# Two attention units to a TensorE visit, a second way of decoding three more weight pieces, and a new table of ranks

## The chip, the cores and the metric

The kernel runs on one core of one Trainium2 chip. The metric is the device time of one execution in microseconds (us), as the median of several executions. An execution's profile gives a span, which runs from the program's first instruction to its last; what lies around the span adds some two microseconds to the time. Five engines run their own instruction streams in order: TensorE (PE), VectorE (DVE), ScalarE (ACT), GpSimd (POOL) and SyncE (SP), which issues the DMAs. Weight loads of TensorE are shown as PEld.

## What is computed

The reference has two stages. The first is softmax attention with a mask: a query sees the first `n_global` keys and its own last `n_local` keys. The second is a mixer: one small network across tokens, then one across channels, each with a residual.

```python
# batch, heads, seq, head_dim = 4, 8, 768, 64;  n_global, n_local = 8, 96
scores = scale * np.matmul(q, k.transpose(0, 1, 3, 2))
keep = is_global | is_local
scores = np.where(keep, scores + bias[None], -1000000000.0)
a = np.exp(scores - np.max(scores, axis=-1, keepdims=True))
a = a / (np.sum(a, axis=-1, keepdims=True) + 1e-09)
attn = np.matmul(a, v)
# the attention output, heads side by side: x[batch, 768, 512]
h = np.maximum(x.transpose(0, 2, 1) @ w_tok1, 0.0) @ w_tok2     # 768 -> 256 -> 768
u = x + h.transpose(0, 2, 1)
out = u + np.maximum(u @ w_ch1, 0.0) @ w_ch2                    # 512 -> 1536 -> 512
```

All arrays are float32 except the four weight matrices, which arrive as 64-bit floats and have to be turned into 32-bit ones on the chip.

## The kernel before

**Units.** The attention is cut into 48 units, 12 to a batch. A unit `v` is two heads (`e` = 0, 1) and 256 query rows. Its place in the batch gives `j` = 0, 1 or 2, the third of the sequence, four units each. Because of the mask a unit with `j` = 0 meets 256 keys in all, and one with `j` = 1 or 2 meets 384. The steps of a unit are planned in `pair` (L389):

- `load` brings the unit's packed q, k and v into one of four ring buffers (SP), and `q` scales q (POOL from the second batch on).
- `S` makes the scores (PE, tile `sp`): eight passes in the trace, with a contraction of only 64 rows, so that the two heads use the two halves of the array's rows ("64*128").
- `max` adds the bias and finds row minima of the negated scores (DVE), `exp` is the exponential (ACT), `sum` and `inv` are the reciprocal, `norm` multiplies (POOL).
- For units before the twentieth, `T` transposes on PE (tile `tp`) and `back` copies the result out of PSUM. From the twentieth on (`FAR`), `split` (DVE) sorts 16-bit halves apart, `turn` is a DMA transpose issued by SP, and `join` (DVE or ACT) sorts the halves together again.
- `V` multiplies with the values (PE, tile `op`), eight passes for `j` = 0 and twelve otherwise, with the two heads in the two halves of the array's columns ("128*64"); `put` copies to `x` (ACT).

**Token mixing** of a batch (`tokens`, L543) takes all of its units. In the third and fourth batch each of six row blocks `s` goes through `xs` (DVE), `xt` (a DMA transpose), `xw` (DVE), `nh` (ACT), `nl` (DVE) and `J` (PE, tile `pj`). After the sixth come `jh` (ACT) and `jl` (DVE) for two halves, and then eight steps `U` (PE, tile `pu`), each followed by `ua`, `uh` and `ul`, which make the high and low part of `u`.

**Channel mixing** (`channel`, L660) is most of TensorE's work: for each batch 24 steps `F` (tile `hp`, twelve matmuls of 384 columns) and 24 steps `G` (tile `acc`, twelve matmuls, planned as two halves `G..0` and `G..1`), 12 for each half of the sequence. Each product is made of three matmuls of high and low parts. `fh` (ACT) and `fl` (DVE) stand between `F` and `G`.

**Weights** (`weights`, L288) come in 30 pieces of 512 columns, six for the token network and 24 for the channel network; step `F` with number f below 12 needs pieces up to 6+2f, step `G` up to 7+2f. A piece is decoded by `down` (ACT), then either `shift`, `upper`, `lower` (three on DVE), or, for a piece number from `BYTES` on, `last` (ACT), `ends` and `lower` (two on DVE); then `high` (ACT) and `low` (POOL or DVE).

**Order.** No engine's order is written out. `Plan` (L95) is a list scheduler that runs when the program is built: each step has a planned cost, the steps it waits for, buffers and PSUM banks it takes and gives, and a rank (`rank`, L762). When an engine is free in the plan, it takes the ready step of lowest rank; TensorE adds a penalty (`TURN`) when the form of the matmuls changes. The steps are then recorded in this order, and on the chip each engine runs in it. So a changed rank, cost or rule moves steps on all engines. The channel mixing of batch b−1 is what TensorE does between the attention visits of batch b; the channel mixing of the last batch has nothing beside it.

```python
 512  [f"load{v}"] if v > 1 else [], r - 8, ["q"])
 ...
 515  add(f"S{v}", "pe", 0.86 if j else 0.65, scores, ...
 540  add(f"V{v}", "pe", 0.86 if j else 0.65, values, ...
```

Every operation is recorded through one helper (`InOrder`, L197), so that nearly all rows of the profile say L205, and tiles tell them apart.

Of the kernel before, what the change touches and what calls it, by code (L numbers as in the profile page):

```python
# [21 lines left out]
B, H, S, D = 4, 8, 768, 64  # L22
# [6 lines left out]
NF = FF // P  # L29
# [13 lines left out]
DOWN = 2.0 ** -112  # L43
BYTES = 12

# [168 lines left out]
class Fast:  # L214
# [3 lines left out]
    def __init__(self, ctx, tc, early, pk, nb, w1, w2, wc1, wc2, out):  # L218
# [8 lines left out]
        def pool(name, bufs, **kw):  # L227
            return ctx.enter_context(tc.tile_pool(name=name, bufs=bufs, **kw))

        const = self.const = pool("const", 1)  # L230

        self.ring = early.slots + [const.tile([P, 1024], F32, tag=f"r{i}", name=f"e{i}") for i in range(RING - 3)]
        self.prep = pool("prep", 2)
        self.soft = pool("soft", 8)
# [13 lines left out]
        self.A, self.Z = {}, {}  # L248
        self.plan = Plan(dict(w=2 * NF, raw=AHEAD, t=3, p=6, mix=4, nat=3, q=1, x=8, u0=8, u1=8, hl=6), BUSY,
                         dict(dve=self.dve, act=self.act, pool=self.pool))  # L250
# [138 lines left out]
    def pair(self, v):  # L389
# [122 lines left out]

        add(f"S{v}", "pe", 0.86 if j else 0.65, scores, ([f"q{v}"] if v else []) + ([f"ul{b - 1}7"] if b > 1 else []), r,
            [("sp", v, 0), ("sp", v, 1)], ["q"], "rows")
        for e in range(2):
            add(f"max{v}{e}", "dve", 0.7 if j else 0.57, lambda e=e: maxima(e), [f"S{v}"] + ([f"max{v}0"] if e else []),
                r - 10, wp if e == 0 else [], [("sp", v, e)])
            add(f"exp{v}{e}", "act", 1.0 if j else 0.89, lambda e=e: exps(e), [f"max{v}{e}"], r)
# [511 lines left out]
```

## Time and profile before

| | us |
|---|---|
| median of three executions | 616.7 (616.03 to 617.36) |
| the profiled execution | 617.54 |
| its span | 615.7 |

| engine | busy us | share of the span |
|---|---|---|
| DVE | 359.4 | 58% |
| ACT | 275.2 | 45% |
| POOL | 209.6 | 34% |

A row of the profile gives the engine, the operation, the tile that it writes and those it reads, the number of instructions and their time. In the timeline the first two columns are the start and the duration in us. Ends of matmuls are modelled by the profiler and overlap their successors, so the distance between starts is what tells the pace of TensorE. Idle time that an engine spent before an instruction stands in brackets, with what ended it.

### The profile page before, as it was taken

Reading aid. Unit: us, or ns where it says so; the run is one execution under the profiler, and the core shown is the slowest. Engines: PE = TensorE matmul, PEld = TensorE weight load, DVE = VectorE, ACT = ScalarE, POOL = GpSimd, SP = SyncE. Lnnn points to the kernel's source line nnn. Section 1 sums busy time; section 2 is a strip of 40 time slices with the busy share of each in tenths; the row PEclk is TensorE's granted clock in tenths of the full one; section 3 lists DMA queues with packets and bytes.
Section 4 is the critical chain, followed back from the end, with each engine's and each line's share of the span. In section 5 each row is a group of like instructions: output and inputs, shape, how many; then the busy total and the mean of one; then the engine's idle time right before and its main releaser. Section 6 shows DMA issues by size and latency. Waiting matters only on the chain.

```text
span 615.7 us, 10478 instructions
## 1 busy us (share of the span) xinstructions
PE 597.7 (97%) x3730; PEld 543.1 (88%) x3730; DVE 359.4 (58%) x921; ACT 275.2 (45%) x736; POOL 209.6 (34%) x319
## 2 busy tenths in 40 slices
PE   5899999899999999999999999999999999999996
PEld 3577798899998999888989999898988999999996
DVE  4999999986453417557774466676655354113112
ACT  5999968864362205446652333355423231111110
POOL 4898665773130204434321034362222124000000
PEclk9999999999999999999999999999999999999999
DMA  7971571613352001667965103457541301001001
GB/s 252 400 241 33 192 253 28 248 36 120 84 107 84 1 0 52 124 150 148 206 149 96 38 27 77 122 137 164 162 78 35 61 14 39 0 1 53 0 1 56
DMA packets 84028, 62.63 MB, mean 102 GB/s; under 512 B 69760, under 2 KB 73984, under 8 KB 83968
## 3 DMA queue, kind: packets, MB, share of 16 engines
q1 hardware_dynamic: 83968, 61.88, 37.1%
q8 instruction: 31, 0.51, 0.4%
q14 instruction: 29, 0.24, 0.1%
HBM read 38.80 MB, written 6.29 MB: 73 GB/s over the span
## 4 chain that ended last, share of the span: by engine, by line
PE 81%; DVE 7%; POOL 6%; issue 3%; DMA 1%; ACT 1%; SPq 0%; DVEq 0%; POOLq 0%
PE acc L205 29%; PE hp L205 29%; PE sp L205 6%; PE pj L205 5%; PE op L205 5%; PE pu L205 5%; POOL pp L205 3%; DVE t L205 2%; DVE w L205 2%; POOL wc L205 2%; PE tp L205 1%; DMA p<-r 1%; DVE pp L205 1%; DMA e<-pk 1%; PE xtp L205 1%
## 5 line engine op out<-in xcount | busy, mean ns | idle before, releaser
L205 PE MATMUL hp<-uh,wc 128*128 128x384 f32 x768 | 210.6, 336 | 2.3 <-POOL wc L205 1.8
L205 PE MATMUL acc<-hh,wc 128*128 128x384 f32 x768 | 198.9, 339 | 0.0
L205 PEld LDWEIGHTS hp<-uh,wc 128*128 128x128 f32 x768 | 139.6, 188 | 5.6 <-POOL wc L205 2.8
L205 PEld LDWEIGHTS acc<-hh,wc 128*128 128x128 f32 x768 | 136.6, 188 | 9.0 <-issue 8.4
L205 ACT ACTIVATE hh<-hp 128x384 fp32r<-128x384 f32 x96 | 46.9, 489 | 206.9 <-PE hp L205 194.8
L205 PE MATMUL acc<-hl,wc 128*128 128x384 f32 x384 | 128.8, 336 | 0.4 <-DVE hl L205 0.2
L205 PE MATMUL hp<-ul,wc 128*128 128x384 f32 x384 | 128.4, 334 | 0.0
L205 DVE SCALAR_TENSOR_TENSOR hl<-hp,hh 128x384 fp32r<-128x384 f32 x96 | 53.0, 552 | 127.8 <-ACT hh L205 125.8
L205 POOL TENSOR_SCALAR p<-p,st 128x256 f32<-128x256 f32 (+1 forms) x132 | 74.3, 581 | 69.2 <-DVE st L205 53.0
L205 DVE COPY r<-p 128x1024 uint16<-128x1024 uint16 (+1 forms) x90 | 65.0, 732 | 37.8 <-DMA p<-r 17.6
L205 ACT ACTIVATE p<-p,st 128x256 f32<-128x256 f32 (+1 forms) x132 | 63.6, 485 | 21.5 <-DVE st L205 21.5
L205 PEld LDWEIGHTS acc<-hl,wc 128*128 128x128 f32 x384 | 72.1, 188 | 1.0 <-DVE hl L205 1.0
L205 PEld LDWEIGHTS hp<-ul,wc 128*128 128x128 f32 x384 | 72.1, 188 | 0.0
L205 POOL TENSOR_TENSOR ul<-x,uh 128x384 fp32r<-128x384 f32 x25 | 26.9, 1085 | 103.6 <-ACT uh L205 82.9
L205 POOL TENSOR_SCALAR qs<-e,sc 128x256 f32<-128x256 f32 x36 | 22.1, 615 | 106.2 <-DMA e<-pk 71.7
L205 PE MATMUL sp<-e,qs 64*128 64x256 f32 (+1 forms) x304 | 39.3, 387 | 0.2 <-POOL qs L205 0.2
L205 POOL TENSOR_TENSOR wc<-t,wc 128x512 fp32r<-128x512 f32 x20 | 32.1, 1612 | 17.3 <-ACT wc L205 17.3
L205 POOL TENSOR_SCALAR pp<-pp,st 128x256 f32<-128x256 f32 (+1 forms) x60 | 35.8, 613 | 4.3 <-DVE st L205 4.2
L205 ACT COPY r<-p 128x1024 uint16<-128x1024 uint16 (+1 forms) x22 | 29.1, 1322 | 10.3 <-DMA p<-r 6.4
L205 PEld LDWEIGHTS sp<-e,qs 64*128 64x128 f32 x304 | 25.8, 193 | 8.3 <-issue 4.3
L205 ACT ACTIVATE pp<-pp,st 128x256 f32<-128x256 f32 (+1 forms) x60 | 28.5, 484 | 2.5 <-DVE st L205 2.5
L205 ACT COPY x<-op 128x256 f32<-128x256 f32 (+1 forms) x64 | 18.6, 319 | 24.4 <-PE op L205 24.1
(99 smaller groups left out, 779.9 us busy)
## 6 DMA issues: line engine op xcount, KB each, us to landing
w<-wc SPq DMA_DIRECT2D x24, 512.0 KB, 5.3
e<-pk SPq DMA_DIRECT2D x24, 512.0 KB, 3.9
out<-o SPq DMA_DIRECT2D x32, 192.0 KB, 1.9
e<-pk SPq DMA_DIRECT2D x13, 384.0 KB, 3.6
unit<-pk SPq DMA_DIRECT2D x8, 512.0 KB, 9.5
w<-w SPq DMA_DIRECT2D x6, 512.0 KB, 9.8
p<-r SPq DMA_TRANSPOSE x56, 3.1
unit<-pk SPq DMA_DIRECT2D x2, 384.0 KB, 3.6
```

What stands on the lines that cost most here:

```text
L205: ins = getattr(self.engine, name)(*args, **kw)
```

## The change

The change has five parts.

1. `TWINS = 24`: from unit 24 on, which is the third batch, an even unit's `S` and the following odd unit's `S` become one visit. The even one waits for both units' `q` and takes all four PSUM banks, and the odd one waits only for it, with rank −1000, so that it comes right behind. The same is done with `V`: the even unit's waits for all four `join` steps of the two units, and the odd one follows. To keep the odd unit's steps in a fixed order behind the even one's, `max`, `split`, `turn` and `join` of the odd unit wait for those of the even one.
2. Scaled queries get three buffers (`prep`, `q=2` in the plan) in place of two (`q=1`).
3. `BYTES` goes from 12 to 9: pieces 9, 10 and 11 are decoded by `last`, `ends` and `lower` in place of `shift`, `upper` and `lower`.
4. The planned cost of `lower`, `LOWER`, goes from 1.05 to 1.3.
5. The ranks are set anew: pairs, weights and channel steps.

```diff
+TWINS = 24
-BYTES = 12
+BYTES = 9
...
-        self.prep = pool("prep", 2)
+        self.prep = pool("prep", 3)
...
-        self.plan = Plan(dict(w=2 * NF, raw=AHEAD, t=3, p=6, mix=4, nat=3, q=1, x=8, u0=8, u1=8, hl=6), BUSY,
+        self.plan = Plan(dict(w=2 * NF, raw=AHEAD, t=3, p=6, mix=4, nat=3, q=2, x=8, u0=8, u1=8, hl=6), BUSY,
...
+        twins = [v] if v < TWINS else [v, v + 1] if v % 2 == 0 else []
...
-        add(f"S{v}", "pe", 0.86 if j else 0.65, scores, ([f"q{v}"] if v else []) + ([f"ul{b - 1}7"] if b > 1 else []), r,
-            [("sp", v, 0), ("sp", v, 1)], ["q"], "rows")
+        add(f"S{v}", "pe", 0.86 if j else 0.65, scores,
+            ([f"q{x}" for x in twins if x] + ([f"ul{b - 1}7"] if b > 1 else [])) if twins else [f"S{v - 1}"], r if twins else -1000,
+            [("sp", x, e) for x in twins for e in range(2)], ["q"], "rows")
...
-            add(f"max{v}{e}", ..., [f"S{v}"] + ([f"max{v}0"] if e else []),
+            add(f"max{v}{e}", ..., [f"S{v}"] + ([f"max{v}0"] if e else [] if twins else [f"max{v - 1}1"]),
...
-                add(f"turn{v}{e}", "sp", 1.9, lambda e=e: turned(e), [f"split{v}{e}"], -1000)
+                add(f"turn{v}{e}", "sp", 1.9, lambda e=e: turned(e), [f"split{v}{e}"] + ([] if twins else [f"turn{v - 1}{e}"]), -1000)
...
-        add(f"V{v}", "pe", 0.86 if j else 0.65, values, [f"{late}{v}0", f"{late}{v}1"], r - 10,
-            [("op", v)] + (["w"] if v < H // 2 else ["x"] if b and j < 2 else []), give, "columns")
+        xs = len(twins) * (["w"] if v < H // 2 else ["x"] if b and j < 2 else [])
+        add(f"V{v}", "pe", 0.86 if j else 0.65, values, [f"{late}{x}{e}" for x in twins for e in range(2)] or [f"V{v - 1}"],
+            r - 10 if twins else -1000, [("op", x) for x in twins] + xs, give, "columns")
...
-        return 40.0 + 12.0 * at[0] if at[0] < 6 else 100 + 10 * at[0]
+        return 40.0 + 12.0 * at[0] if at[0] < 6 else 100 + 8 * at[0]
...
-UPPER, LOWER, LOW = 0.85, 1.05, dict(dve=0.64, pool=1.45)
+UPPER, LOWER, LOW = 0.85, 1.3, dict(dve=0.64, pool=1.45)
```

What the new table of ranks and the new rules make of the order is seen in the built programs. The rows are an engine's instructions in order, without times; one more line at the file's top makes L205 into L206.

The first place is TensorE at the first visits of the third batch. `e_58`, `e_59` and `e_60` are the ring buffers of units 24, 25 and 26. Before:

```order
L205 MATMUL acc<-hl,wc 128x384
L205 MATMUL sp<-e_58,qs 128x128 x2
L205 MATMUL sp<-e_58,qs 128x256 x2
L205 MATMUL acc<-hh,wc 128x384 x2
L205 MATMUL acc<-hl,wc 128x384
L205 MATMUL acc<-hh,wc 128x384 x2
L205 MATMUL acc<-hl,wc 128x384
L205 MATMUL sp<-e_59,qs 128x128 x2
L205 MATMUL sp<-e_59,qs 128x256 x2
L205 MATMUL sp<-e_60,qs 128x128 x2
L205 MATMUL sp<-e_60,qs 128x256 x2
```

And of the change:

```order
L206 MATMUL hp<-uh,wc 128x384
L206 MATMUL sp<-e_58,qs 128x128 x2
L206 MATMUL sp<-e_58,qs 128x256 x2
L206 MATMUL sp<-e_59,qs 128x128 x2
L206 MATMUL sp<-e_59,qs 128x256 x2
L206 MATMUL acc<-hh,wc 128x384 x2
```

Unit 25's scores now stand directly behind unit 24's. Counted over the third and fourth batch, the attention takes 24 visits of TensorE in the new order, twelve for scores and twelve for values, and no visit holds both.

The second place is TensorE at the end of the token mixing of the third batch. `e_216` is the ring buffer of unit 35, the batch's last. Before, `V35` is followed by `G440`, `G441`, `F46`, `G450`, `G451` and `F47`; from the last row of `F47` on:

```order
L205 MATMUL hp<-uh,wc 128x384
L205 MATMUL pj<-ph,w1h 128x512
...
L205 MATMUL pj<-pl,w1h 128x512
L205 MATMUL acc<-hh,wc 128x384 x2
L205 MATMUL acc<-hl,wc 128x384
...
L205 MATMUL acc<-hl,wc 128x384
L205 MATMUL pu<-w2h,ph 128x384
```

Of the change, from `V35` on:

```order
L206 MATMUL op<-r,e_60 64x128 x4
L206 MATMUL op<-r,e_216 64x256 x2
L206 MATMUL op<-r,e_216 64x128 x4
L206 MATMUL hp<-uh,wc 128x384
...
L206 MATMUL acc<-hl,wc 128x384
L206 MATMUL pj<-ph,w1h 128x512
...
L206 MATMUL pj<-pl,w1h 128x512
L206 MATMUL pu<-w2h,ph 128x384
```

Before, the 18 matmuls of `G460`, `G461` and `G470` stand between `J25` and `U20`. Now all channel steps of the second batch stand ahead of `J23`: `F47`, `G460`, `G461`, `G470` and `G471` are all that is left between `V35` and `J23`, and nothing stands between `J23`, `J24`, `J25` and `U20`.

The third place is VectorE at the decoding of pieces 23 and 24. The rows that write `w` are `ends`, those that write `t` from `t` and `w` are `lower`. Before, where `w_1546` is piece 23 and `w_1612` piece 24:

```order
L205 SCALAR_TENSOR_TENSOR w_1546<-w_1546 128x512
L205 SCALAR_TENSOR_TENSOR t_1636<-t_1636,w_1546 128x512
L205 SCALAR_TENSOR_TENSOR hl<-hp,hh 128x384
L205 SCALAR_TENSOR_TENSOR w_1612<-w_1612 128x512
L205 SCALAR_TENSOR_TENSOR t_1660<-t_1660,w_1612 128x512
```

Of the change, where `w_1566` is piece 23 and `w_1586` piece 24:

```order
L206 SCALAR_TENSOR_TENSOR w_1566<-w_1566 128x512
L206 SCALAR_TENSOR_TENSOR t_1652<-t_1652,w_1566 128x512
L206 SCALAR_TENSOR_TENSOR hl<-hp,hh 128x384
L206 TENSOR_SCALAR st<-st 128x4
L206 RECIPROCAL st<-st 128x4
L206 SCALAR_TENSOR_TENSOR w_1586<-w_1586 128x512
L206 ISA p,st<-sp,be 128x256
...
L206 TENSOR_TENSOR wc<-t_1652,wc 128x512
L206 SCALAR_TENSOR_TENSOR t_1668<-t_1668,w_1586 128x512
```

The maxima (`ISA`) of units 17, 18 and 19, which stood at the last piece or behind it, now stand among pieces 22 to 26, and `low` of pieces 23, 24 and 26 has moved from POOL to DVE. In the other direction `low` of pieces 9 and 14 has moved from DVE to POOL. On TensorE `T17`, `S19`, `T18`, `V17`, `V18` and `G100`, which stood behind `F11`, now stand ahead of it.

More of the change, by code (lines that the diff above doesn't have):

```diff
@@ L511, in pair @@
         wp = ["w"] if wide else ["p", "p"]
-        add(f"S{v}", "pe", 0.86 if j else 0.65, scores, ([f"q{v}"] if v else []) + ([f"ul{b - 1}7"] if b > 1 else []), r,
-            [("sp", v, 0), ("sp", v, 1)], ["q"], "rows")
+        add(f"S{v}", "pe", 0.86 if j else 0.65, scores,
+            ([f"q{x}" for x in twins if x] + ([f"ul{b - 1}7"] if b > 1 else [])) if twins else [f"S{v - 1}"], r if twins else -1000,
+            [("sp", x, e) for x in twins for e in range(2)], ["q"], "rows")
         for e in range(2):
-            add(f"max{v}{e}", "dve", 0.7 if j else 0.57, lambda e=e: maxima(e), [f"S{v}"] + ([f"max{v}0"] if e else []),
+            add(f"max{v}{e}", "dve", 0.7 if j else 0.57, lambda e=e: maxima(e), [f"S{v}"] + ([f"max{v}0"] if e else [] if twins else [f"max{v - 1}1"]),
                 r - 10, wp if e == 0 else [], [("sp", v, e)])
@@ L532, in pair @@
             for e in range(2):
-                add(f"split{v}{e}", "dve", 0.68 if j else 0.54, lambda e=e: split(e), [f"norm{v}{e}"] + ([f"split{v}0"] if e else []), r - 10,
+                add(f"split{v}{e}", "dve", 0.68 if j else 0.54, lambda e=e: split(e), [f"norm{v}{e}"] + ([f"split{v}0"] if e else [] if twins else [f"split{v - 1}1"]), r - 10,
                     [] if e else ["mix", "mix"])
-                add(f"turn{v}{e}", "sp", 1.9, lambda e=e: turned(e), [f"split{v}{e}"], -1000)
-                add(f"join{v}{e}", dict(act=1.26 if j else 0.96, dve=0.68 if j else 0.54), 0, lambda en, e=e: join(e, en), [f"turn{v}{e}"], r - 10, (), ["p"])
+                add(f"turn{v}{e}", "sp", 1.9, lambda e=e: turned(e), [f"split{v}{e}"] + ([] if twins else [f"turn{v - 1}{e}"]), -1000)
+                add(f"join{v}{e}", dict(act=1.26 if j else 0.96, dve=0.68 if j else 0.54), 0, lambda en, e=e: join(e, en), [f"turn{v}{e}"] + ([] if twins else [f"join{v - 1}{e}"]), r - 10, (), ["p"])
             late, give = "join", ["mix", "mix"]
-        add(f"V{v}", "pe", 0.86 if j else 0.65, values, [f"{late}{v}0", f"{late}{v}1"], r - 10,
-            [("op", v)] + (["w"] if v < H // 2 else ["x"] if b and j < 2 else []), give, "columns")
+        xs = len(twins) * (["w"] if v < H // 2 else ["x"] if b and j < 2 else [])
+        add(f"V{v}", "pe", 0.86 if j else 0.65, values, [f"{late}{x}{e}" for x in twins for e in range(2)] or [f"V{v - 1}"],
+            r - 10 if twins else -1000, [("op", x) for x in twins] + xs, give, "columns")
         add(f"put{v}", "act", 0.34 if j == 1 else 0.28, put, [f"V{v}"], r - 15, (), [("op", v)])
@@ L774, in rank @@
         if b == 0:
-            return 10.0 * v
+            return 11.0 * v
         if b == 1:
-            return 140 + 8.5 * i
-        return BATCH * b - 60 + 8.5 * i
+            return 130 + 8.5 * i
+        return BATCH * b - 70 + 8.5 * (i // 2 * 2) + 1.0 * (i % 2)
     if kind == "mix":
@@ L785, in rank @@
         b, k = divmod(at[0], 2 * NF)
-        return 140 + 5.0 * k if b == 0 else BATCH * b + 100 + 5.5 * k
+        return 130 + 5.0 * k if b == 0 else BATCH * b + 100 + 5.5 * k
 BATCH = 140.0
-UPPER, LOWER, LOW = 0.85, 1.05, dict(dve=0.64, pool=1.45)
+UPPER, LOWER, LOW = 0.85, 1.3, dict(dve=0.64, pool=1.45)
 @with_exitstack
```

## Prediction

> **What bounds the kernel now.** I read the page first: which engine is full, and where in the span.
>
> ```profile
> PE 597.7 (97%) x3730; PEld 543.1 (88%) x3730; DVE 359.4 (58%) x921; ACT 275.2 (45%) x736; POOL 209.6 (34%) x319
> PE   5899999899999999999999999999999999999996
> ```
>
> TensorE is busy from the second slice of forty to the end. So the time can fall in two ways only: TensorE gets less to do, or it stands still less. Next, the busy times by stretch, for who feeds it, and what TensorE waited for.
>
> ```profile
> 105.00:120.00 15.00, 14.45 (x92) 13.45 (x89) 14.37 (x16) 11.99 (x24) 10.36 (x7) 1.00 0.69 247
> 340.00:360.00 20.00, 20.00 (x116) 18.69 (x115) 7.86 (x13) 4.88 (x9) 0.00 (x0) 1.00 0.13 30
> PE hp L205 <- POOL wc L205: 1.8, 2, 1.3
> PE sp L205 <- POOL qs L205: 0.2, 1, 0.2
> ```
>
> The columns behind the length are PE, PEld, DVE, ACT and POOL, then the granted clock, which is full. From 105 to 120 us VectorE is as full as TensorE: it decodes the channel weights, and TensorE runs close behind it. In 340 to 360 VectorE is at 39%. TensorE's waits are few: behind the weights (`wc`), and once for a scaled query. Waiting is almost all gone already; what is left is in the work, and there the matmuls of all kinds stay the same in number. The change can only act on what lies between them.
>
> **What a visit costs.** In the stream of `hp` and `acc` matmuls one starts every 0.173 us (288.00 to 288.18 and so on). I take the distance from the last stream matmul before a visit to the third after it, less three of these, 0.52. Five visits in the timeline of TensorE; first one unit's scores, then two units' values:
>
> ```profile
> 271.26 0.34 PE L205 MATMUL hp<-uh,wc 128*128 128x384 f32 x1
> 271.53 1.14 PE L205 MATMUL sp<-e,qs 64*128 64x256 f32 x8
> ...
> 273.05 0.34 PE L205 MATMUL acc<-hl,wc 128*128 128x384 f32 x1
> ```
>
> ```profile
> 186.64 0.34 PE L205 MATMUL hp<-uh,wc 128*128 128x384 f32 x1
> 186.90 1.96 PE L205 MATMUL op<-r,e 128*64 128x256 f32 x24
> ...
> 189.25 0.34 PE L205 MATMUL acc<-hl,wc 128*128 128x384 f32 x1
> ```
>
> Values and then scores in one visit, of one unit each, and with a second unit's scores:
>
> ```profile
> 288.00 0.33 PE L205 MATMUL hp<-ul,wc 128*128 128x384 f32 x1
> 288.18 0.34 PE L205 MATMUL hp<-uh,wc 128*128 128x384 f32 x1
> 288.44 1.09 PE L205 MATMUL op<-r,e 128*64 128x256 f32 x12
> 289.46 1.13 PE L205 MATMUL sp<-e,qs 64*128 64x256 f32 x8
> ...
> 290.98 0.34 PE L205 MATMUL acc<-hl,wc 128*128 128x384 f32 x1
> ```
>
> ```profile
> 276.70 0.34 PE L205 MATMUL hp<-uh,wc 128*128 128x384 f32 x1
> 276.97 1.09 PE L205 MATMUL op<-r,e 128*64 128x256 f32 x12
> 277.99 2.00 PE L205 MATMUL sp<-e,qs 64*128 64x256 f32 x16
> ...
> 280.37 0.34 PE L205 MATMUL acc<-hl,wc 128*128 128x384 f32 x1
> ```
>
> And one unit's values alone, the last of the third batch:
>
> ```profile
> 341.67 0.34 PE L205 MATMUL hp<-uh,wc 128*128 128x384 f32 x1
> 341.94 1.09 PE L205 MATMUL op<-r,e 128*64 128x256 f32 x12
> 342.96 0.62 PE L205 MATMUL acc<-hh,wc 128*128 128x384 f32 x2
> 343.41 0.35 PE L205 MATMUL acc<-hl,wc 128*128 128x384 f32 x1
> ```
>
> One unit's scores alone take 1.79−0.52 = 1.27, one unit's values alone 1.74−0.52 = 1.22, two units' values 2.61−0.52 = 2.09, values and scores in one visit 2.80−0.52 = 2.28, values and two units' scores 3.67−0.52 = 3.15. A second unit of values adds 0.87, a second unit of scores 3.15−2.28 = 0.87. So a visit costs 0.40 (scores) or 0.35 (values) beside its work, and where it holds both kinds, 2.28−2×0.87 = 0.54, which is 0.17 more than the mean of 0.37. The Trainium skill has a rule for this (TensorEngine Tiling (Array Packing), section Key Properties): a change of the tiling mode drains TensorE. By it the step from values to scores, rows halved after columns halved, is a full change like going in or out, and if going in and out takes 0.37 together, it would take about half of that, 0.18; the trace has 0.17 and agrees.
>
> **Third and fourth batch: −4.7, and −0.5.** In the timeline I count 32 visits there, from unit 24's scores at 239.66 to unit 47's values at 485.68, ten of them with both kinds. The new order has 24, none mixed. That is 8×0.37 + 10×0.17 = 3.0+1.7 = 4.7 less. The wait for `qs` also goes: 0.2 by its row and, with the refill behind it, 0.5, since the order puts the scores further behind their loads and a third buffer frees `q`. This is certain in the count and tight in the size: between 4 and 5.5.
>
> **Second batch: +1.1.** The new ranks split visits there. From `V14` on I count seven with four mixed before, and ten with three mixed now: 3×0.37 − 0.17 = +0.9; with the values of three units (21, 22, 23) now alone I take 1.1.
>
> **End of the third batch: +3.2, a wait that the change adds.** The token mixing of this batch hangs on its last unit. Before:
>
> ```profile
> 348.64 0.69 DVE L205 TENSOR_TENSOR pl<-xw,ph 128x512 fp32r<-128x512 f32 x1
> ...
> 350.69 0.69 DVE L205 TENSOR_TENSOR pl<-xw,ph 128x512 fp32r<-128x512 f32 x1 [0.69 <-ACT ph L205]
> ...
> 352.83 0.69 DVE L205 TENSOR_TENSOR pl<-xw,ph 128x512 fp32r<-128x512 f32 x1
> 355.68 1.37 DVE L205 SCALAR_TENSOR_TENSOR pl<-pj,ph 128x512 fp32r<-128x512 f32 x2 [2.15 <-ACT ph L205]
> ```
>
> On TensorE meanwhile, the start of `J25` and that of `U20`:
>
> ```profile
> 354.17 0.39 PE L205 MATMUL pj<-ph,w1h 128*128 128x512 f32 x1
> ...
> 358.68 0.33 PE L205 MATMUL pu<-w2h,ph 128*128 128x384 f32 x1
> ```
>
> `V35` ends at 342.96. The low parts that `J23`, `J24` and `J25` need are there at 349.33, 351.38 and 353.52: 6.4, 8.4 and 10.6 later. `J25` starts at 354.17, and `jl` ends at 357.05, 2.9 later; `U20` starts only at 358.68, so none of it was waited for. In the new order `F47` and `G460` to `G471` give TensorE 36×0.173 = 6.24 behind `V35`, and the three `J` (0.23 a matmul, 1.39 each) would end at 10.4. But `J25` may start at 10.6 and `U20` at 10.6+2.9 = 13.5. That is 3.1 of standing still, and 0.1 to refill: 3.2. What is queued behind is all of TensorE's work, since `U20` stands at the head of its queue and no channel step of the second batch is left as cover. Bounds: 2.4, if the transpose of unit 34's rows, now earlier than unit 35's, pulls the chain ahead, and 4.5 if the two collide on SP. In the fourth batch `F70` to `G700` (42×0.173 = 7.3) stand behind `V47`, and `G710`, `G711` ahead of `U30`; that covers 6.4 and 2.9, and I add nothing.
>
> **Weights: −1.0.** `ends` and `lower` for three more pieces take the place of `shift`, `upper` and `lower`:
>
> ```profile
> L205 DVE SCALAR_TENSOR_TENSOR t<-w,t 128x512 int32<-128x512 int32 x24 | 20.0, 834 | 0.3
> L205 DVE SCALAR_TENSOR_TENSOR t<-t,w 128x512 int32<-128x512 int32 x18 | 19.2, 1069 | 1.3
> L205 DVE SCALAR_TENSOR_TENSOR w<-w 128x512 int32<-128x512 int32 x18 | 18.9, 1049 | 0.0
> L205 DVE TENSOR_SCALAR t<-t 128x512 int32<-128x512 int32 x12 | 6.6, 551 | 0.0
> L205 ACT ACTIVATE w<-w 128x512 int32<-128x512 uint8 x18 | 11.9, 671 | 0.0
> L205 DVE CUSTOM_DVE_ANT_0 p<-sp,be 128x256 f32<-128x256 f32 x48 | 20.1, 419 | 12.0 <-PE sp L205 11.9
> L205 DVE TENSOR_TENSOR wc<-t,wc 128x512 fp32r<-128x512 f32 x4 | 3.6, 898 | 0.0
> ```
>
> VectorE pays 1.05+1.07 = 2.12 a piece in place of 0.55+2×0.83 = 2.22; three pieces give 0.3. ACT pays 3×0.67 = 2.0 more, where the row above has it at 11.99 of 15. Together with two low parts that go to POOL, pieces 13 to 21 come some 1.2 to 2 us sooner. That removes the small gaps of TensorE from 90 to 115 us (four in the timeline, 2.0 in all). The last eight pieces come later. By piece 24 VectorE has eight maxima (8×0.42 = 3.4) and a low part (0.9) more, less the lead, so about 3; by piece 27 four maxima and two low parts on top, so about 6.5. TensorE, too, has more ahead of `F11`: `T17`, `T18`, `S19`, `V17`, `V18` and `G100`: 1.27 + 2.09 + 6×0.173 = 4.4, and 16 transposes of 128 columns, at a third of 0.173 at the least 0.9, so 5.3 or more. So the wait at `F9` for piece 24, the larger of the two in the row of waits (1.3), stays about as it is, and I give back 1.0 at the pieces behind it. Bounds: −3, if VectorE's order holds all the way, and +4 (below). The start up to `U00` I leave at zero: VectorE, ACT and POOL have within 0.5 us of the same work ahead of it, in another order. I allow 1.5 either way.
>
> **What I cost at nothing.** The loads of a twin now wait for both units' values, one visit. Least room have units 30 and 31: `G300`, the scores of 28 and 29, `G301`, `F32` and `G310`, `G311` lie between, 36×0.173+2.1 = 8.4. A load lands 3.9 after its issue:
>
> ```profile
> e<-pk SPq DMA_DIRECT2D x24, 512.0 KB, 3.9
> ```
>
> Two `q` on POOL, each under a microsecond, follow, so 2 to 3 us are over. Without that cover it is a wait of `sp`. On SP a load can stand behind a `turn` that waits for VectorE, which in these stretches has half of its time free. The planned costs and the ranks act through the order alone.
>
> **Sum.** −4.7 −0.5 +1.1 +3.2 −1.0 = −1.9. The profiled execution took 617.54, so 615.6; the median before is 616.7, and I forecast **614.8**.
>
> **Rivals.**
>
> *The last weight pieces fall behind (slower).* The place is `F9` to `F11`. For it speaks the row of 105 to 120: VectorE is full, and ACT gets twelve exponentials among these pieces too. The price: if VectorE's 6.5 us at piece 27 meet only 2.5 of the 5.3 that TensorE has more, because `S17` to `S19` themselves come late, TensorE stands for 4 more, and the time is 618.8. It decides from 3.1 us of added standing on (−1.9+3.1 = +1.2). Against it: TensorE gets the extra work from the same order. A rule of the Trainium skill (SBUF — State Buffer, section Who interferes with whom) speaks for it: VectorE and GpSimd share a pair of ports under an exclusive lock, and the loser blocks for a whole instruction. By it the `norm` of units 17 and 18, now among these pieces, would block VectorE's two-input steps as `low` does now; the row below, one `ends` of 1.78 where their mean is 1.05, agrees, and six such collisions would be 4.4, the same place and price.
>
> ```profile
> 88.99 1.78 DVE L205 SCALAR_TENSOR_TENSOR w<-w 128x512 int32<-128x512 int32 x1
> ```
>
> *The start gains more.* If the pieces are sooner all along, all of TensorE's gaps behind the weights go (nine in the timeline from 84.08 to 129.31, 4.6 with their refills): 616.7−4.7−0.5+1.1+3.2−4.6 = 611.2.
>
> *The twins wait (no change).* A twin's values wait for eight more steps of one chain. If every one of the 12 value visits stood 0.2, 2.4 of the 4.7 would go: 617.2. Against it: in the order 36 stream matmuls and a visit of scores stand twice between unit 24's scores and its values, some 16 us, and now, with `S36` and `S37` side by side already, no `op` waits in these batches.
>
> **Chances.** The forecast 0.50 (613.3 to 616.3), the last pieces 0.18, the better start 0.15, waiting twins 0.17. A measurement of this kernel can tell about 0.2%, 1.2 us, from no change: 615.5 to 617.9. Of the forecast's 0.50 a third lies above 615.5. Faster: 0.33+0.15 = 0.48; within: 0.17+0.13 = 0.30; slower: 0.18+0.04 = 0.22. The range leaves out half of the better start and the far end of the last pieces: 611.8 to 618.6.
>
> **What would show it.** Right: 24 visits in the last two attention batches with starts as above; `pu` of the third batch behind an idle 2.4 to 4.5, ended by VectorE's `pl`; idle time behind `wc` about 3 in all. Wrong: idle before `hp` behind `wc` of over 5 around 125 to 140, or `sp` and `op` rows with idle time before them after 240.

## The result, and the profile after

| | median us | runs |
|---|---|---|
| before | 616.7 (616.03 to 617.36) | 4 |
| after | 612.58 (610.93 to 613.36) | 4 |

The ratio of after to before is 0.9938, with a 95% interval of 0.9925 to 0.995: faster by 0.6%. The profiled execution of after took 610.93, its span is 609.2. First the new page's row of engines and its row of TensorE over the span's 40 slices, then the rows of TensorE's waits (times in us: in total, how often, the longest):

```profile
PE 594.4 (98%) x3730; PEld 544.1 (89%) x3730; DVE 359.6 (59%) x930; ACT 268.1 (44%) x733; POOL 204.4 (34%) x313
PE   6899999999999999999999999999999999999996
```

```profile
PE warm L206 <- issue: 3.9, 1, 3.9
...
PE hp L206 <- POOL wc L206: 0.6, 1, 0.6
...
PE pj L206 <- ACT ph L206: 0.4, 2, 0.2
```

The number of TensorE's instructions is the same, and it is busy for 3.3 us less (597.7 before). The fixed price of visits counts as busy in this row: of the kernels with added visits below, the one with 16 single visits is busy for 3.7 us more (616.4 for 612.7) than the one that holds the same matmuls in eight. Of what it waited for behind the weights (`wc`: 1.8 from POOL and 0.5 from VectorE before) 0.6 is left, and `pj` waits, which it did not before. `warm <- issue` is the beginning of the program, ahead of the first matmul: 3.9 here and 5.4 in the profiled execution of before. These 1.5 us belong to the one execution, not to the kernel (last section), so I compare from the first `U` of the first batch, `U00`, to the last matmul: 539.1 before, 533.6 after, 5.4 less (the two are rounded). From the first scores to `U00` it was 65.0 and 65.4.

**Visits.** Two visits of twins in the timeline of after, scores and values, with their neighbours in the stream:

```profile
258.11 0.34 PE L206 MATMUL acc<-hl,wc 128*128 128x384 f32 x1
258.38 2.00 PE L206 MATMUL sp<-e,qs 64*128 64x256 f32 x16
...
260.76 0.34 PE L206 MATMUL acc<-hl,wc 128*128 128x384 f32 x1
...
340.61 0.34 PE L206 MATMUL acc<-hl,wc 128*128 128x384 f32 x1
340.87 1.96 PE L206 MATMUL op<-r,e 128*64 128x256 f32 x24
...
343.22 0.51 PE L206 MATMUL hp<-uh,wc 128*128 128x384 f32 x2
```

By the measure of the prediction the values take 343.22−340.61−0.52 = 2.09. The scores take 260.76−258.11−0.52 = 2.13. All 24 visits of the last two batches look like this, none is mixed, and no `sp` or `op` waits in them.

**The end of the third batch.** TensorE from `J23` to `U20`, as the timeline has it; a `J` matmul starts 0.23 after the last where nothing holds it:

```profile
350.29 0.40 PE L206 MATMUL pj<-pl,w1h 128*128 128x512 f32 x1
350.85 0.49 PE L206 MATMUL pj<-ph,w1h 128*128 128x512 f32 x1 [0.16 <-ACT ph L206]
351.18 0.40 PE L206 MATMUL pj<-ph,w1l 128*128 128x512 f32 x1
351.57 0.50 PE L206 MATMUL pj<-pl,w1h 128*128 128x512 f32 x1
...
352.37 0.40 PE L206 MATMUL pj<-pl,w1h 128*128 128x512 f32 x1
352.96 0.50 PE L206 MATMUL pj<-ph,w1h 128*128 128x512 f32 x1 [0.19 <-ACT ph L206]
353.30 0.40 PE L206 MATMUL pj<-ph,w1l 128*128 128x512 f32 x1
353.69 0.50 PE L206 MATMUL pj<-pl,w1h 128*128 128x512 f32 x1
...
354.49 0.39 PE L206 MATMUL pj<-pl,w1h 128*128 128x512 f32 x1
354.93 0.45 PE L206 MATMUL pu<-w2h,ph 128*128 128x384 f32 x1
355.21 0.34 PE L206 MATMUL pu<-w2l,ph 128*128 128x384 f32 x1
355.66 0.45 PE L206 MATMUL pu<-w2h,pl 128*128 128x384 f32 x1
```

The gaps beyond the pace are 0.33, 0.16, 0.36, 0.16, 0.21 and 0.28: 1.5 in all. Behind each stop the next start is 0.11 late as well (350.85 to 351.18 is 0.33 in place of 0.23); there are seven of these, 0.8 more, so 2.3 in all. `J24`, `J25` and `U20` each stop twice: ahead of the matmul that reads the high part (`ph`), and ahead of the one that reads the low part (`pl`). VectorE made the low parts meanwhile:

```profile
348.73 0.69 DVE L206 TENSOR_TENSOR pl<-xw,ph 128x512 fp32r<-128x512 f32 x1 [0.73 <-ACT ph L206]
...
350.82 0.69 DVE L206 TENSOR_TENSOR pl<-xw,ph 128x512 fp32r<-128x512 f32 x1 [0.73 <-ACT ph L206]
...
352.94 0.69 DVE L206 TENSOR_TENSOR pl<-xw,ph 128x512 fp32r<-128x512 f32 x1 [0.76 <-ACT ph L206]
354.91 1.32 DVE L206 SCALAR_TENSOR_TENSOR pl<-pj,ph 128x512 fp32r<-128x512 f32 x2 [1.28 <-ACT ph L206]
```

The low parts of `J23` to `J25` end 6.6, 8.7 and 10.8 after the end of `V35` at 342.83, and `U20` starts 12.1 after it.

**Behind the weights.** The busy times of after, for 105 to 120 us and for 120 to 135 (PE, PEld, DVE, ACT, POOL behind the length), and behind them the second stretch of before:

```profile
105.00:120.00 15.00, 15.00 (x97) 13.50 (x96) 13.13 (x32) 13.63 (x35) 9.06 (x10) 1.00 0.47 161
120.00:135.00 15.00, 15.00 (x106) 13.68 (x106) 12.61 (x28) 12.18 (x32) 11.08 (x11) 1.00 0.01 3
```

```profile
120.00:135.00 15.00, 13.70 (x87) 11.84 (x86) 13.56 (x33) 12.46 (x34) 10.94 (x10) 1.00 0.22 70
```

TensorE now stands nowhere between 105 and 135; before it stood for 0.55 and 1.30 us there. VectorE, which was full from 105 to 120 (14.37 of 15), has 1.9 us free.

### The profile page after: what moved, and what is told of

Its sections match the earlier page's. It is cut to its first block, busy times and chain, and to the rows that moved or that the text cites. A ratio compares the mean times of both kernels' runs of the same rounds, so it can differ in the third digit from the quotient of the medians.

```text
span 609.2 us, 10441 instructions
## 1 busy us (share of the span) xinstructions
PE 594.4 (98%) x3730; PEld 544.1 (89%) x3730; DVE 359.6 (59%) x930; ACT 268.1 (44%) x733; POOL 204.4 (34%) x313
## 4 chain that ended last, share of the span: by engine, by line
PE 85%; DVE 6%; POOL 4%; issue 2%; ACT 2%; DMA 0%; SPq 0%; DVEq 0%; ACTq 0%; POOLq 0%
PE acc L206 31%; PE hp L206 31%; PE op L206 6%; PE sp L206 6%; PE pu L206 5%; PE pj L206 4%; DVE pp L206 2%; POOL wc L206 1%; PE tp L206 1%; DVE t L206 1%; POOL pp L206 1%; ACT pp L206 1%; PE xtp L206 1%; POOL p L206 1%; POOL ul L206 0%
## 5 line engine op out<-in xcount | busy, mean ns | idle before, releaser
L206 PE MATMUL hp<-uh,wc 128*128 128x384 f32 x768 | 211.3, 336 | 0.6 <-POOL wc L206 0.6
L206 PE MATMUL acc<-hh,wc 128*128 128x384 f32 x768 | 197.9, 338 | 0.0
L206 PEld LDWEIGHTS acc<-hh,wc 128*128 128x128 f32 x768 | 137.3, 188 | 6.8 <-issue 5.2
L206 PEld LDWEIGHTS hp<-uh,wc 128*128 128x128 f32 x768 | 139.9, 188 | 3.5 <-issue 1.4
L206 ACT ACTIVATE hh<-hp 128x384 fp32r<-128x384 f32 x96 | 47.0, 489 | 198.7 <-PE hp L206 197.0
L206 DVE SCALAR_TENSOR_TENSOR hl<-hp,hh 128x384 fp32r<-128x384 f32 x96 | 53.1, 553 | 136.9 <-ACT hh L206 136.7
L206 PE MATMUL acc<-hl,wc 128*128 128x384 f32 x384 | 128.5, 335 | 0.0
L206 PE MATMUL hp<-ul,wc 128*128 128x384 f32 x384 | 128.4, 334 | 0.0
L206 POOL TENSOR_SCALAR p<-p,st 128x256 f32<-128x256 f32 (+1 forms) x132 | 81.4, 636 | 48.0 <-ACT p L206 20.3
L206 DVE COPY r<-p 128x1024 uint16<-128x1024 uint16 (+1 forms) x96 | 67.7, 723 | 41.2 <-DMA p<-r 16.7
L206 ACT ACTIVATE p<-p,st 128x256 f32<-128x256 f32 (+1 forms) x132 | 63.5, 484 | 30.3 <-DVE st L206 16.9
L206 POOL TENSOR_SCALAR qs<-e,sc 128x256 f32<-128x256 f32 x36 | 19.3, 538 | 157.4 <-DMA e<-pk 138.2
L206 PEld LDWEIGHTS hp<-ul,wc 128*128 128x128 f32 x384 | 72.1, 188 | 0.1
L206 PEld LDWEIGHTS acc<-hl,wc 128*128 128x128 f32 x384 | 72.1, 188 | 0.0
L206 POOL TENSOR_TENSOR ul<-x,uh 128x384 fp32r<-128x384 f32 x21 | 22.9, 1096 | 69.9 <-ACT uh L206 68.1
L206 PE MATMUL sp<-e,qs 64*128 64x256 f32 (+1 forms) x304 | 38.2, 382 | 0.1
L206 POOL TENSOR_SCALAR pp<-pp,st 128x256 f32<-128x256 f32 (+1 forms) x60 | 33.1, 571 | 3.8 <-DVE st L206 3.5
L206 PEld LDWEIGHTS sp<-e,qs 64*128 64x128 f32 x304 | 26.7, 193 | 8.2 <-issue 3.3
L206 POOL TENSOR_TENSOR wc<-t,wc 128x512 fp32r<-128x512 f32 x19 | 29.8, 1575 | 12.2 <-ACT wc L206 12.2
L206 ACT COPY x<-op 128x256 f32<-128x256 f32 (+1 forms) x64 | 18.6, 317 | 29.1 <-PE op L206 28.7
L206 ACT ACTIVATE pp<-pp,st 128x256 f32<-128x256 f32 (+1 forms) x60 | 28.3, 475 | 1.1 <-DVE st L206 1.0
L206 ACT CAST uh<-x 128x384 fp32r<-128x384 f32 x32 | 16.1, 515 | 27.3 <-DVE x L206 24.6
```

What stands on the lines that cost most here:

```text
L206: ins = getattr(self.engine, name)(*args, **kw)
```

## The experiments

The second column is the time of all runs, the third their ratio to the kernel before on the same chip, the fourth what the profiled execution took from `U00` to the last matmul. Verdicts within 0.2% rest on the trace.

| kernel | median us | ratio, 95% interval | `U00` to the last matmul |
|---|---|---|---|
| before | 616.7 | | 539.1 |
| after | 612.58 | 0.9938 (0.9925 to 0.995) | 533.6 |
| twins, old ranks | 620.83 | 1.0083 (1.0063 to 1.0104) | 542.4 |
| no twins | 614.93 | 0.9976 (0.9965 to 0.9987) | 537.1 |
| BYTES = 12 | 612.98 | 0.9947 (0.9928 to 0.9967) | 534.6 |
| low parts first | 613.74 | 0.9958 (0.9943 to 0.9973) | 534.7 |
| 16 single visits added | 631.94 | 1.0245 (1.0219 to 1.027) | 555.1 |
| 8 double visits added | 629.57 | 1.0206 (1.018 to 1.0231) | 551.8 |
| 8 mixed visits added | 630.27 | 1.0228 (1.0199 to 1.0258) | 552.0 |
| the same in 16 visits | 632.35 | 1.0245 (1.0217 to 1.0273) | 553.8 |
| before with BYTES = 9 | 616.38 | 0.9995 (0.9983 to 1.0008) | 538.6 |
| before with a third query buffer | 619.22 | 1.0043 (1.0028 to 1.0058) | 539.0 |
| before with rank step 8 | 614.88 | 0.9972 (0.996 to 0.9984) | 538.0 |
| more cover | 609.74 | 0.9888 (0.9871 to 0.9905) | 531.7 |

### Does a visit have a fixed price, and a mixed one another?

Four kernels add visits to the last channel mixing, where TensorE has nothing but its stream. The first two hold the same matmuls in 16 visits and in eight, and the last two hold theirs in eight and in 16.

```diff
+                what = "S" if 76 <= k < 92 else ""
...
+                    add(f"D{k}", "pe", 1.0 * len(what), lambda k=k, what=what: extra(k, what), [f"G{k}0"], -1000,
+                        [("dm", k, 0), ("dm", k, 1)], [("dm", k, 0), ("dm", k, 1)], "rows")
```

In the other three `what` is `"" if k % 2 else "SS"`, `"" if k % 2 else "VS"` and `"S" if k % 2 else "V"`; `extra` runs one unit's score or value matmuls on what the ring still holds.

> The new kernel with 16 added visits of one unit's scores each (the eight matmuls... of a unit with j of 1 or more: four of 64x128 by 64x256; their results are read by nothing), one between the two halves of G76 to G91, where TensorE otherwise has only its stream. Theory (a visit costs 0.40 beside its work of 0.87): 16 x 1.27 = +20.3 against the new kernel, 632.9, and 3.2 more than eight visits of two. Rival (no fixed price; what I read as one is the latency of the last matmuls, hidden or not by their number): the same as eight visits of two.

> The same added matmuls as in the kernel with 16 single visits, in eight visits of two units' scores, in G76, G78 to G90. Theory: 8 x (0.40 + 2 x 0.87) = +17.1 against the new kernel, 629.7. Rival: as long as with 16 single visits.

> The new kernel with eight added visits that hold one unit's values and then one unit's scores (their results are read by nothing), in G76, G78 to G90. Theory: 8 x (0.54 + 2 x 0.87) = +18.2 against the new kernel, 630.8. Rival (the step from values to scores inside a visit costs nothing): 8 x (0.37 + 2 x 0.87) = +16.9, 629.5.

> The matmuls of the eight mixed visits in 16 visits: one unit's values in G76, G78 to G90, one unit's scores in G77, G79 to G91. Theory: 8 x (0.35 + 0.87) + 8 x (0.40 + 0.87) = +19.9 against the new kernel, 632.5, so 1.7 more than the mixed ones. Rival (a mixed visit costs as much as two): the same as the mixed ones.

One visit of each kind in the timelines (tile `dm`), of the first three kernels, with the stream matmul ahead and the third one behind:

```profile
527.12 0.34 PE L206 MATMUL acc<-hl,wc 128*128 128x384 f32 x1
527.39 1.14 PE L206 MATMUL dm<-e,qs 64*128 64x256 f32 x8
...
528.91 0.34 PE L206 MATMUL acc<-hl,wc 128*128 128x384 f32 x1
```

```profile
528.26 0.34 PE L206 MATMUL acc<-hl,wc 128*128 128x384 f32 x1
528.53 2.00 PE L206 MATMUL dm<-e,qs 64*128 64x256 f32 x16
...
530.91 0.34 PE L206 MATMUL acc<-hl,wc 128*128 128x384 f32 x1
```

```profile
525.37 0.34 PE L206 MATMUL acc<-hl,wc 128*128 128x384 f32 x1
525.64 1.09 PE L206 MATMUL dm<-e 128*64 128x256 f32 x12
526.65 1.14 PE L206 MATMUL dm<-e,qs 64*128 64x256 f32 x8
...
528.17 0.34 PE L206 MATMUL acc<-hl,wc 128*128 128x384 f32 x1
```

Less 0.52 each, one unit's scores take 1.27, two units' 2.13, values and scores 2.28. In the fourth kernel values alone take 1.22 and scores alone 1.27. A second unit's scores add 0.85, so a visit of scores has a fixed price of 0.42. Values and scores in one visit take 1.27+1.22−2.28 = 0.21 less than in two. Within a kernel the visits agree to 0.002 us. From `U00` on, 16 single visits take 3.3 longer than eight double ones (0.41 a visit), and the values and scores apart 1.8 longer than mixed (0.23 a visit); I had 3.2 and 1.7. By the medians it is 2.4 and 2.1. The fixed price, and its part for the step inside a mixed visit, are shown; the rivals are out. The Trainium skill (TensorEngine Tiling (Array Packing), section Key Properties) states the drain at a change of the tiling mode without a figure; that sharing a visit saves it agrees with these rows.

### Twins without the new order, and the new order without twins

The first kernel is the one before with the twins, their buffer and the pair ranks that they need; its edit is shown against the new kernel. The second is the new one with `TWINS = 48`.

```diff
-BYTES = 9
+BYTES = 12
...
-        return ... 100 + 8 * at[0]
+        return ... 100 + 10 * at[0]
...
-            return 11.0 * v
+            return 10.0 * v
...
-            return 130 + 8.5 * i
+            return 140 + 8.5 * i
...
-        return 130 + 5.0 * k if b == 0 else ...
+        return 140 + 5.0 * k if b == 0 else ...
...
-UPPER, LOWER, LOW = 0.85, 1.3, ...
+UPPER, LOWER, LOW = 0.85, 1.05, ...
```

> The kernel before with nothing but the twins: TWINS = 24, the third query buffer, and the rank of pairs from the third batch on (without it the planner finds no order); BYTES, LOWER and all other ranks as before. The order then has the 24 unmixed visits of the new kernel in the last two batches, and seven visits with four mixed in the second, as before; behind V35 come J23, J24, J25 and U20 with no channel step between them. Theory (a visit costs 0.37, a mixed one 0.17 more; the token mixing of the third batch needs 12.1 us from V35's end to U20, as in the new kernel's trace): visits -4.4, U20 waits 12.1-4.2 = 7.9 in place of 0, so +3.5 against before, 620.2. Rival (the twins bring the gain by themselves, and what TensorE has no work for at the batch's end is short, as the 1.5 us of the new kernel): -4.4+1.5, 613.8.

It is 620.83, where my theory had 620.2 and the rival 613.8. The twins alone make the kernel slower by 0.8%. The end of the third batch in its timeline:

```profile
349.69 1.96 PE L206 MATMUL op<-r,e 128*64 128x256 f32 x24
357.67 0.79 PE L206 MATMUL pj<-ph,w1h 128*128 128x512 f32 x1 [6.02 <-ACT ph L206]
...
364.07 0.44 PE L206 MATMUL pu<-w2h,ph 128*128 128x384 f32 x1
```

`U20` starts 12.4 after the end of `V35` at 351.65, of which the three `J` are 4.2 of work at full pace: 8.2 go that no channel step fills, and the visits' gain is lost in them. From `U00` on this kernel takes 8.8 longer than the new one. Counted as time beyond the pace of the matmuls, 7.1 of it lie behind `U10`, where the cover is missing, and 1.7 between `U00` and `U10`, where the weights are decoded. So what the new ranks bring beside the twins is for the most part the cover behind `V35`.

> The new kernel with TWINS = 48, so no unit shares its visit by rule; all else as in the new kernel. The order has 29 visits with nine mixed in the last two batches (24 and none in the new kernel), and channel steps stand between the J of the third batch's end and U20. Theory (fixed price of a visit): 5 x 0.37 + 9 x 0.17 = +3.4 for the visits, -1.5 for the wait before U20, so +1.9 against the new kernel, 614.5. Rival (the start brings all of the gain, and the twins give theirs back at the end of the batch): within 0.5 of the new kernel, 612.6.

It is 614.93, 2.4 above the new kernel, nearer to the theory (+1.9) than to the rival (0). From `U00` on it is 3.5 longer. The visits of the last two batches take 47.9 in place of 44.7, +3.3 (I had 3.4; eight of these visits are mixed, and the one that holds values, scores and values counts twice in my nine), and those of the second batch 24.1 in place of 23.5, which is no more than two executions of one order differ by (below). The 1.5 before `U20` are gone, but waits of about 0.9 in the fourth batch are new.

### Why the wait before `U20` is 1.5 and not 3.2

```diff
-                for n, (w, i) in enumerate(((0, 0), (1, 0), (0, 1))):
+                for n, (w, i) in enumerate(((0, 1), (0, 0), (1, 0)) if b == 2 else ((0, 0), (1, 0), (0, 1))):
...
-                for p, w in ((0, 0), (0, 1), (1, 0)):
+                for p, w in ((1, 0), (0, 0), (0, 1)) if b == 2 else ((0, 0), (0, 1), (1, 0)):
```

> The new kernel, but in the token mixing of the third batch the matmuls that read the low part of the rows (pl) come first in each J and in each U, not last. Theory (the wait before U20 is 1.5 and not the 3.2 that I worked out because each J and U begins with the high part, whose chain is 0.7 us shorter, and works while the low part is made): each of J23 to U20 now waits for its low part, the standing at the end of the third batch grows from 1.5 to about 3.2, +1.7 against the new kernel, 614.3. Rival (the low parts were not what came last, or VectorE was simply faster than worked out): no change, 612.6.

```profile
342.20 1.96 PE L206 MATMUL op<-r,e 128*64 128x256 f32 x24
...
355.19 0.50 PE L206 MATMUL pj<-pl,w1h 128*128 128x512 f32 x1 [0.43 <-DVE pl L206]
...
357.63 0.44 PE L206 MATMUL pu<-w2h,pl 128*128 128x384 f32 x1 [0.78 <-DVE pl L206]
```

Now the low part ends each wait (`<-DVE pl`), and `U20` starts 13.5 after the end of `V35` (344.16), the very figure that I had worked out for the new kernel. The gaps are 2.7 in place of 1.5; from `U10` to `U20` it takes 1.5 longer, but 0.3 of it comes back behind the start of `U20`, and from `U00` on it is 1.1 longer where I had 1.7. The median is 1.2 above the new kernel's, which is less than these few runs can tell alone. So the prediction's chain was right in length, and it was wrong in what must wait for it: of the matmuls of each `J` and `U` only every third needs the low part.

### More cover

```diff
-                        ... [f"G{k - 1}1"] if k else []), r,
+                        ... [f"G{k - 1}1"] if k else []) + (["V34"] if (k, i) == (45, 0) else ["J25"] if (k, i) == (47, 1) else []), r,
...
-                    ... + ([f"F{k - 1}"] if k else []),
+                    ... + ([f"F{k - 1}"] if k else []) + (["V34"] if k == 47 else []),
...
-                ... + ([f"J{b}{s - 1}"] if s else []),
+                ... + ([f"J{b}{s - 1}"] if s else []) + (["G470"] if (b, s) == (2, 3) else []),
...
-                [f"jl{b}0", ...
+                (["G471"] if b == 2 and not i else []) + [f"jl{b}0", ...
```

> The new kernel, with V34 and V35 put ahead of G450, G451 and F47, and G471 between J25 and U20: 42 stream matmuls stand between V35 and J23 (36 in the new kernel), and six more ahead of U20, so 8.3 us of stream in place of 6.2 cover the chain of 12.1. Theory (the 1.5 us of standing before U20 are the chain less its cover): the gaps there fall to 0.5 or less, -1.0, 611.6, and V34, issued 2.1 sooner, still finds its join made (it ended 2.0 ahead of V34), or waits 0.2. Rival (the chain shifts with what DVE and SP have beside it, or V34 waits for its join by as much as the gap falls): 612.6.

```profile
339.37 1.09 PE L206 MATMUL op<-r,e 128*64 128x256 f32 x12
340.62 0.65 PE L206 MATMUL op<-r,e 128*64 128x256 f32 x4 [0.16 <-DVE hl L206]
...
354.08 0.33 PE L206 MATMUL acc<-hl,wc 128*128 128x384 f32 x1
354.26 0.33 PE L206 MATMUL pu<-w2h,ph 128*128 128x384 f32 x1
```

No gap is left from `J23` to `U20`. `V35` waits 0.16, but not for its join: in the timeline of VectorE the last join ends at 337.91, and the row names the step `fl` (tile `hl`), which ends at 340.56. From `U00` on this kernel takes 1.9 less than the new one, 1.2 of it from `U10` to `U20` and 0.6 behind it, most of them stops inside `U20` that are gone; I had 1.0. Its time is 609.74 (608.19 to 610.94), 1.1% below the kernel before. That is the fastest of these kernels. How it stands to the new kernel was not run side by side: the intervals against before do not overlap (0.9871 to 0.9905, 0.9925 to 0.995). The medians differ by 2.8, of which the traces explain 1.9.

### What brought the weights forward

Four kernels change one part each. The first is the new kernel, the others are the one before.

```diff
-BYTES = 9
+BYTES = 12
```

> The new kernel with BYTES = 12: pieces 9 to 11 are decoded as before, on the new ranks. Theory (the smaller gaps behind the weights come from the new order of the pieces and units, the moved last bits only shift 0.1 us of VectorE a piece): within 1 of the new kernel, 612.6, and the gaps of TensorE from U00 to U10 stay below 4 us. Rival (the moved last bits bring them): the gaps are back at 6.3, 616.1. The second batch has eight visits with six mixed in this order, ten with three in the new kernel: -0.2 by the price of visits.

```diff
-BYTES = 12
+BYTES = 9
```

> The kernel before with BYTES = 9 alone: ScalarE finds the last bits of 21 pieces in place of 18. Theory (it frees 0.1 us of VectorE a piece, and the run with BYTES = 12 on the new ranks stood 3.3 us behind the weights between U00 and U10 against the new kernel's 2.9): TensorE's gaps there fall by no more than 1 from 6.4, 616 or a little less. Rival (these last bits carry the 3.5 us that the new kernel gained behind the weights): gaps near 2.9, 613.

```diff
-        self.prep = pool("prep", 2)
+        self.prep = pool("prep", 3)
...
-  nat=3, q=1, ...
+  nat=3, q=2, ...
```

> The kernel before with the third query buffer alone. Theory (in the run with the old ranks, the old BYTES and the third buffer the gaps behind the weights were 4.6 where the kernel before has 6.4): gaps about 4.6, that is -1.8; the wait for qs goes, -0.5; 30 visits with 13 mixed in the last two batches in place of 32 with ten, -0.2; together -2.5, 614.0. Rival (the buffer only serves the twins): 616.5.

```diff
-        return ... 100 + 10 * at[0]
+        return ... 100 + 8 * at[0]
```

> The kernel before with the step of the weights' rank of 8 in place of 10 alone, so that the planner wants the later pieces sooner. The last three batches keep the visits and the order of before. Theory (the ranks bring the rest of what was gained behind the weights): gaps between U00 and U10 of 4 to 5 in place of 6.4, 615. Rival (no step of it by itself does anything): 616.5.

From `U00` to `U10` I add up, in each timeline, what TensorE took beyond its stream's pace, since a wait may stand in front of a stream matmul or of a visit:

| kernel | visits, with waits ahead of them | gaps in the stream | both |
|---|---|---|---|
| before | 22.5 | 6.4 | 28.9 |
| before with BYTES = 9 | 24.7 | 4.0 | 28.7 |
| before with a third query buffer | 23.4 | 4.7 | 28.1 |
| before with rank step 8 | 23.8 | 4.3 | 28.1 |
| after with BYTES = 12 | 24.0 | 3.3 | 27.2 |
| after | 23.5 | 2.9 | 26.4 |

On the kernel before, the three parts alone each take 1.7 to 2.4 from the gaps, but each gives much of it back at a visit; with `BYTES` = 9 nearly all (616.38 against 616.47 before on the same chip: no difference). In two of them my theory was wrong. With `BYTES` = 9 the time stayed, as I had it, but the gaps fell by 2.4 where I had at most 1. Of the 4.0 that are left, 1.6 are no waits but late starts at half the clock, behind a visit with two pauses (last section); without them the gaps are 2.4, below the 2.9 of the new kernel, as the rival had it. With the third buffer the gaps fell as expected but the time did not: 619.22, slower by 0.4%, where I had 614.0. There the profiled execution, 617.73, took 1.1 longer than that of before up to `U00` and the same from it on; what else its median holds is open. The rank step is the one part that pays alone: 614.88, expected 615; its waits of TensorE behind the weights are down to 0.6, as in the new kernel. In the new order, three pieces less of `last` and `ends` cost 0.4 in the gaps, and 612.98 against 612.58 in the medians, which do not tell it from nothing. The sums of the last column are good to about 1 only: seven profiled executions of kernels that are the same up to `U10` (after, the four with added visits, low parts first, more cover) have gaps of 2.7 to 2.9, but 23.5 or 24.5 at the visits. So what is shown is that ScalarE's last bits do not carry the time gained: alone they change nothing, and without them the new order keeps all but 0.4 of it by the medians, 0.8 by this table. The rank of the weights brings part of it. The planned cost of `lower` and the other ranks were not run alone, and how the rest of the new order adds up stays open.

## Why the prediction was right or wrong

The forecast, 614.8, was 2.2 us too long: TensorE lost less at two places than I had worked out. Term by term, in us, by the traces (by the medians the sum is −4.1):

| term | prediction | measured |
|---|---|---|
| visits of batches three and four | −4.7 | −4.7 |
| the wait for `qs` | −0.5 | −0.5 |
| visits of the second batch | +1.1 | +1.0 |
| end of the third batch | +3.2 | +2.3 |
| weights | −1.0 | −3.5 |
| up to `U00` | 0 ± 1.5 | +0.4 |
| sum (of the terms before rounding) | −1.9 | −5.1 |

**Visits of the last two batches, and the wait for `qs`: right.** In the visits TensorE took 48.93 before and 44.66 after, 4.3 less. Behind each visit the next starts are 0.11 late in all, 32 times before and 24 times after, which is 0.9 less. Together that is 5.2, as the two terms have it. The visit with the wait for `qs`, at 427.68, took 0.50 longer than the visit of the same matmuls at 276.97. Count, kinds and starts are as forecast, and the fixed price is shown by the added visits.

**Second batch: right**, 22.5 to 23.5.

**End of the third batch: the step "`J25` may start at 10.6 and `U20` at 10.6+2.9 = 13.5" failed.** The low parts came when I had said (6.6, 8.7 and 10.8 for 6.4, 8.4 and 10.6), but I let each `J` start only when its low part was there, and `U20` only when both `jl` were. Both begin with the high part, so that TensorE works while the low part is made. So it lost 2.3, stops of 1.5 ahead of both parts and 0.8 in late starts behind them, and the sign that I had named, an idle of 2.4 to 4.5 ahead of `pu` ended by `pl`, did not come. With the low part first the 13.5 came out as worked out; with more cover the wait went to 0, and with none 8.2 went into it. My lower bound, 2.4, did not allow for this.

**Weights: the mechanism was seen, the size was wrong.** The step "By piece 24 VectorE has eight maxima (8×0.42 = 3.4) and a low part (0.9) more, less the lead, so about 3" failed, and with it that the wait at `F9` for piece 24 "stays about as it is". Before, that wait was this row; after, the one wait of the stretch is at an earlier piece:

```profile
122.35 0.62 PE L205 MATMUL hp<-uh,wc 128*128 128x384 f32 x2 [1.26 <-POOL wc L205]
```

```profile
100.16 0.61 PE L206 MATMUL hp<-uh,wc 128*128 128x384 f32 x2 [0.62 <-POOL wc L206]
```

Counted from `U00`, piece 24's low part was ready after 52.5 (51.0 before), so VectorE brought it 1.5 later and not 3. TensorE came to `F9` after 53.1 (49.1 before), 4.0 later, behind the visits that the new order puts ahead of it. So the wait went. VectorE's steps were cheaper than their old means:

```profile
L206 DVE SCALAR_TENSOR_TENSOR w<-w 128x512 int32<-128x512 int32 x21 | 19.1, 907 | 0.0
```

`ends` takes 0.91 in the mean where I had put 1.05, a low part 0.79 for 0.90, and the eight maxima went at 0.345 from one to the next, 2.8 for my 3.4. What makes an `ends` long is in the timelines. First one of before with what POOL did meanwhile (`wc`, two low parts; the first ends at 114.74), then one of after, when POOL was idle:

```profile
113.02 3.42 POOL L205 TENSOR_TENSOR wc<-t,wc 128x512 fp32r<-128x512 f32 x2
113.51 1.78 DVE L205 SCALAR_TENSOR_TENSOR w<-w 128x512 int32<-128x512 int32 x1
```

```profile
112.51 0.68 DVE L206 SCALAR_TENSOR_TENSOR w<-w 128x512 int32<-128x512 int32 x1
```

Before, eight of 18 `ends` begin while a low part runs on POOL, and take 0.93 to 1.78; the other ten take 0.67 or 0.68. After, seven of 21 do (0.71 to 1.78), and of the other 14 all but one take 0.66 to 0.69 (1.03, beside another step of POOL with two inputs, `ul`). So the mean of 1.05 was a mixture, 0.68 for most and 1.5 for those that began beside a low part, and the new order mixes it otherwise. How much of the 3.5 each of these changes brings is not shown. `norm` on POOL, which my first rival let collide like a low part, did little: five `ends` beside it took 0.66 to 0.69, and of three `lower` the longest 0.89. The rival of the better start (a gain of 4.6 there) came nearer than my forecast; the twins did not wait, and the last pieces did not fall behind.

## What to carry to other kernels

Count the changes of matmul shape on TensorE, not only its matmuls: here each saved visit of scores was worth 0.42 of fixed price, and a mixed visit 0.21 less than two. Grouping work makes the last group of a stage later as a whole, so look at what is left to run behind it, and if there is nothing, hold work of another stage back for it: against the kernel before, the twins without cover lost 0.8%; with the new order they gained 0.6%, and with two microseconds more of cover 1.1%. When you price a wait on a chain, ask which of the waiting step's instructions reads the chain's end, since the ones ahead of it run meanwhile. And before you price a step by its mean, look whether the mean mixes two cases.

## What the runs showed of the hardware

**A pause lowers TensorE's clock.** In the kernel with the twins and the old ranks TensorE stood for 6.0 us ahead of `J23`. By stretch (the granted clock is the third figure from the end):

```profile
358.00:362.00 4.00, 4.00 (x10) 3.08 (x10) 2.51 (x5) 1.24 (x2) 0.00 (x0) 0.50 0.02 4
362.00:366.00 4.00, 3.89 (x16) 2.54 (x16) 1.92 (x3) 1.20 (x2) 0.00 (x0) 1.00 0.00 0
```

For the next 4 us the granted clock is 0.50, and `J` matmuls start 0.43 apart in place of 0.23. It cost little here (`U20` came 12.4 after `V35`, in the new kernel 12.1), since each `J` had to wait for its low part anyway; with nothing else to wait for, the 18 matmuls would have lost up to 2 us more, by an estimate from their starts (ten of them 0.2 each). The Trainium skill (TensorE: Matmul & The Clock Gate, Part 1: The HAM clock gate (the "warmup" mystery)) has half the clock after an idle window of about 3.4 us, released by a busy one as long; these rows agree, with 0.50 for some 4 us. The waits of the new kernel ahead of `U20`, at most 0.4 each, left the clock full.

It does not take one long pause. In the profiled execution of the kernel before with `BYTES` = 9 the granted clock is 0.50 from 112.6 to 116.0 us, and the stream's matmuls start up to 0.32 apart in place of 0.173. In the 3.4 us ahead of it TensorE stood twice, for 0.73 and 1.00, and otherwise ran eight transposes and two matmuls; no other pause is near:

```profile
110.46 0.66 PE L205 MATMUL tp<-ident,p 128*128 128x128 f32 x4 [0.73 <-DVE hl L205]
112.11 0.44 PE L205 MATMUL hp<-uh,wc 128*128 128x384 f32 x1 [1.00 <-ACT x L205]
```

**The start varies more than the rest.** The profiled executions began their first scores either at 4.8 or at some 6.3 us of the span (the later in the kernel before and in two of those with added visits). From there to `U00` the seven kernels that are the same up to `U10` took 64.8 to 66.6, and from `U00` to `U10` 141.7 to 142.8. From `U10` to `U20`, behind the decoding of the weights, the five of them that have the same order there took 142.9 to 143.0. So nearly all that makes one execution longer than another lies in the first 210 us, and a tenth of a per cent behind them can be read in the trace long before the medians tell it.
